# Retention attention and a SwiGLU FFN on one core: from two stages to six interleaved groups of 512 tokens

## The chip, the cores and the metric

The kernel runs on one NeuronCore of a Trainium2 chip. The metric is device time in microseconds (us) for one execution, lower is better. The engines are PE (TensorE, with its weight loads shown apart as PEld), DVE (VectorE), ACT (ScalarE), POOL (GpSimd) and SP (SyncE, which here only issues DMAs). Each takes its instructions in program order and waits on semaphores for the others.

## The reference

Inputs `q`, `k`, `v` have the shape (4, 8, 768, 64): 4 batches, 8 heads, 768 tokens, 64 per head, all float32. Weights are `w_gate` and `w_val` (512 x 1536), `w_out` (1536 x 512) and `rms_g` (512).

```python
# attention: a decayed linear recurrence per batch and head
gamma = 1.0 - 2.0 ** (-5.0 - np.arange(H))
for t in range(S):
    state = gamma[None, :, None, None] * state + einsum('bhd,bhe->bhde', k[:, :, t], v[:, :, t])
    y[:, :, t] = scale * einsum('bhd,bhde->bhe', q[:, :, t], state)
# x = y with the heads side by side: 3072 tokens x 512
rms = sqrt(mean(x * x, axis=-1, keepdims=True) + 1e-06)
xn = x / rms * rms_g
g = xn @ w_gate
out = (g * sigmoid(g) * (xn @ w_val)) @ w_out
```

The recurrence can be computed in chunks of 128 tokens: inside a chunk as a masked product of q and k with v, across chunks through a 64 x 64 state for each batch and head.

## The kernel before

It has two stages with a weight load between them.

**Attention (lines 96 to 163).** Two loops run over 4 batches and 8 heads. For each of the 32 pairs, SP loads q, k and v of all 768 tokens (192 KB each, in pieces of 256 bytes, lines 105 to 107). DVE scales and casts them to bf16 (L113 to L118), PE transposes q and k two chunks at a time (L126, L130) and DVE copies the results out of PSUM. Then six chunks of 128 tokens follow one another. For each, PE multiplies k and q (`a_ps`, L144), DVE applies the causal mask (`AmT`, L147), PE makes the output from the masked product and from the state (`y_ps`, L150 and L151), ACT copies it into `x_sbuf` (L154), and PE updates the state (`s_ps`, L159 and L160), which ACT scales by gamma^128 into the next `S_sb` (L162). So each chunk's state waits for that of the chunk before through PE and ACT. The matmuls here have 64 or 128 moving columns, and L144, L151 and L159 use 64 of the 128 rows of the array.

**Weights (lines 165 to 183).** The three weight matrices, 9.4 MB of float32, are loaded by SP after the attention loads; DVE casts them to bf16 and folds `rms_g` into the first two.

**FFN (lines 193 to 242).** A loop runs over 24 tiles of 128 tokens. ACT squares and sums (L198) and takes the root (L200), DVE normalises (L204), PE transposes (L209) and DVE copies (L210). For each of three groups of four blocks of d_ff, PE makes gate and value products with 128 moving columns (L220, L225), ACT applies Silu (L230), DVE multiplies (`sgv`, L232), and PE adds four 512-column matmuls to `out_ps` (L235). ACT copies the result (L241) and SP stores it (L242). The order between engines is that of a scheduler over the tile framework.

Of the kernel before, what the change touches and what calls it, by code (L numbers as in the profile page):

```python
# [9 lines left out]
F32 = mybir.dt.float32  # L10
BF16 = mybir.dt.bfloat16
# [6 lines left out]
def kernel(  # L18
# [11 lines left out]
    nc = tc.nc  # L30

    B, H, S, D = q.shape
    assert D == 64
    C = 128
    NCHUNK = S // C
    d_model = H * D
    n_tokens = B * S
    d_ff = moe_w_gate.shape[1]
    n_tiles = n_tokens // 128
    K_SUB = d_model // 128  # L40
    N_SUB = d_ff // 128

    scale = 1.0 / math.sqrt(D)
    gammas = [1.0 - 2.0 ** (-5.0 - h) for h in range(H)]

    const_pool = ctx.enter_context(tc.tile_pool(name="const", bufs=1))

    ident = const_pool.tile([128, 128], BF16)
    make_identity(nc, ident)

    ident_dup = const_pool.tile([D, 2 * D], BF16)
    nc.gpsimd.tensor_copy(ident_dup[:, :D], ident[:D, :D])
    nc.gpsimd.tensor_copy(ident_dup[:, D:], ident[:D, :D])  # L53

    causal = const_pool.tile([128, 128], BF16)
    nc.gpsimd.memset(causal, 1.0)
    nc.gpsimd.affine_select(
        out=causal,
        in_=causal,
        compare_op=mybir.AluOpType.is_ge,  # L60
        fill=0.0,
        base=0,
        pattern=[[1, 128]],
        channel_multiplier=-1,
    )

    iota_i = const_pool.tile([128, 1], mybir.dt.int32)
    nc.gpsimd.iota(iota_i, pattern=[[1, 1]], base=1, channel_multiplier=1)
    iota_f = const_pool.tile([128, 1], F32)
    nc.gpsimd.tensor_copy(iota_f, iota_i)  # L70

    bias_lnscale = const_pool.tile([128, 1], F32)
    nc.gpsimd.memset(bias_lnscale, math.log(scale))
    bias_zero = const_pool.tile([128, 1], F32)
    nc.gpsimd.memset(bias_zero, 0.0)

    gscale_q = const_pool.tile([128, H], F32)
    kscale = const_pool.tile([128, H], F32)
    for h in range(H):
        g = gammas[h]  # L80
        lng = math.log(g)
        nc.scalar.activation(
            gscale_q[:, h:h + 1], iota_f, AF.Exp, scale=lng, bias=bias_lnscale
        )
        nc.scalar.activation(
            kscale[:, h:h + 1], iota_f, AF.Exp, scale=-lng, bias=bias_zero
        )

    x_sbuf = const_pool.tile([128, n_tiles, d_model], BF16)

    NCO = NCHUNK // 2
    with (
        tc.tile_pool(name="work", bufs=5) as work_pool,
        tc.tile_pool(name="psum", bufs=2, space=bass.MemoryType.PSUM) as psum_pool,
    ):
      for b in range(B):
        for h in range(H):
            q_hbm = q[b, h].rearrange("(c p) d -> p c d", p=128)
            k_hbm = k[b, h].rearrange("(c p) d -> p c d", p=128)
            v_hbm = v[b, h].rearrange("(c p) d -> p c d", p=128)  # L100

            q_f = work_pool.tile([128, NCHUNK, D], F32, name="q_f")
            k_f = work_pool.tile([128, NCHUNK, D], F32, name="k_f")
            v_f = work_pool.tile([128, NCHUNK, D], F32, name="v_f")
            nc.sync.dma_start(out=q_f, in_=q_hbm)
            nc.sync.dma_start(out=k_f, in_=k_hbm)
            nc.sync.dma_start(out=v_f, in_=v_hbm)

            gC = gammas[h] ** C
            Qg = work_pool.tile([128, NCHUNK, D], BF16, name="Qg")  # L110
            Kg = work_pool.tile([128, NCHUNK, D], BF16, name="Kg")
            Vb = work_pool.tile([128, NCHUNK, D], BF16, name="Vb")
            nc.vector.tensor_scalar_mul(Qg, q_f, gscale_q[:, h:h + 1])  # L113
            nc.vector.tensor_scalar_mul(Kg, k_f, kscale[:, h:h + 1])
            nc.vector.tensor_copy(Vb, v_f)
            Kgd = work_pool.tile([128, NCHUNK, 2 * D], BF16, name="Kgd")
            nc.vector.tensor_copy(Kgd[:, :, :D], Kg)
            nc.vector.tensor_copy(Kgd[:, :, D:], Kg)  # L118

            Qg2 = Qg.rearrange("p (co c2) d -> p co (c2 d)", c2=2)  # L120
            Kg2 = Kg.rearrange("p (co c2) d -> p co (c2 d)", c2=2)
            QT = work_pool.tile([128, NCO, 128], BF16, name="QT")
            KT = work_pool.tile([128, NCO, 128], BF16, name="KT")
            for co in range(NCO):
                qp = psum_pool.tile([128, 128], BF16, name="qp")
                nc.tensor.transpose(qp, Qg2[:, co, :], ident)  # L126
                nc.vector.tensor_copy(QT[:, co, :], qp)
            for co in range(NCO):
                kp = psum_pool.tile([128, 128], BF16, name="qp")
                nc.tensor.transpose(kp, Kg2[:, co, :], ident)  # L130
                nc.vector.tensor_copy(KT[:, co, :], kp)  # L131

            S_sb = work_pool.tile([128, D], BF16, name="S_sb")
            nc.gpsimd.memset(S_sb, 0.0)

            for c in range(NCHUNK):
                co = c // 2
                po = (c % 2) * 64
                QgT = QT[po:po + 64, co, :]
                KgT = KT[po:po + 64, co, :]  # L140
                S_rhs = S_sb[po:po + 64, :]

                a_ps = psum_pool.tile([128, 128], F32, name="a_ps")
                nc.tensor.matmul(a_ps, KgT, QgT, start=True, stop=True)  # L144

                AmT = work_pool.tile([128, 128], BF16, name="AmT")
                nc.vector.tensor_mul(AmT, a_ps, causal)  # L147

                y_ps = psum_pool.tile([128, D], F32, name="y_ps")
                nc.tensor.matmul(y_ps, AmT, Vb[:, c, :], start=True, stop=False)  # L150
                nc.tensor.matmul(y_ps, QgT, S_rhs, start=False, stop=True)  # L151

                tile_idx = b * NCHUNK + c
                nc.scalar.copy(  # L154
                    x_sbuf[:, tile_idx, h * D:(h + 1) * D], y_ps
                )

                s_ps = psum_pool.tile([128, D], F32, name="s_ps")
                nc.tensor.matmul(s_ps, ident_dup, S_sb[:D, :], start=True, stop=False)  # L159
                nc.tensor.matmul(s_ps, Kgd[:, c, :], Vb[:, c, :], start=False, stop=True)  # L160
                S_new = work_pool.tile([128, D], BF16, name="S_sb")
                nc.scalar.mul(S_new, s_ps, gC)  # L162
                S_sb = S_new

    w_pool = ctx.enter_context(tc.tile_pool(name="weights", bufs=1))
    rms_g_sb = w_pool.tile([128, K_SUB], F32)
    for ks in range(K_SUB):
        nc.sync.dma_start(out=rms_g_sb[:, ks:ks + 1],
                          in_=moe_rms_g[ks * 128:(ks + 1) * 128][:, None])
    wg_f = w_pool.tile([128, K_SUB, d_ff], F32)  # L170
    wv_f = w_pool.tile([128, K_SUB, d_ff], F32)
    wo_f = w_pool.tile([128, N_SUB, d_model], F32)
    nc.sync.dma_start(out=wg_f, in_=moe_w_gate.rearrange("(k p) n -> p k n", p=128))
    nc.sync.dma_start(out=wv_f, in_=moe_w_val.rearrange("(k p) n -> p k n", p=128))
    nc.sync.dma_start(out=wo_f, in_=moe_w_out.rearrange("(n p) m -> p n m", p=128))

    wg_b = w_pool.tile([128, K_SUB, d_ff], BF16)
    wv_b = w_pool.tile([128, K_SUB, d_ff], BF16)
    for s in range(K_SUB):
        nc.vector.tensor_scalar_mul(wg_b[:, s, :], wg_f[:, s, :], rms_g_sb[:, s:s + 1])  # L180
        nc.vector.tensor_scalar_mul(wv_b[:, s, :], wv_f[:, s, :], rms_g_sb[:, s:s + 1])
    wo_b = w_pool.tile([128, N_SUB, d_model], BF16)
    nc.vector.tensor_copy(wo_b, wo_f)

    eps = 1e-6
    eps_tile = w_pool.tile([128, 1], F32)
    nc.gpsimd.memset(eps_tile, eps)

    ffnw = ctx.enter_context(tc.tile_pool(name="ffnw", bufs=4))
    ffnp = ctx.enter_context(tc.tile_pool(name="ffnp", bufs=2, space=bass.MemoryType.PSUM))  # L190
    outp = ctx.enter_context(tc.tile_pool(name="outp", bufs=2, space=bass.MemoryType.PSUM))

    for t in range(n_tiles):
        xt = x_sbuf[:, t, :]

        xsq = ffnw.tile([128, d_model], F32, name="xsq")
        sumsq = ffnw.tile([128, 1], F32, name="sumsq")
        nc.scalar.activation(xsq, xt, AF.Square, accum_out=sumsq)  # L198
        rstd = ffnw.tile([128, 1], F32, name="rstd")
        nc.scalar.activation(rstd, sumsq, AF.Sqrt, scale=1.0 / d_model, bias=eps_tile)  # L200
        nc.vector.reciprocal(rstd, rstd)
# [71 lines left out]
```

## Time and profile before

| | us |
|---|---|
| median of 3 runs (451.76 to 451.96) | 451.9 |
| span of the profiled execution (first to last instruction) | 449.7 |
| PE busy | 380.3 (85%) |
| PE weight loads busy | 247.8 (55%) |
| DVE busy | 209.9 (47%) |
| ACT busy | 191.9 (43%) |
| POOL busy | 6.6 (1%) |

The profile shows one execution. A busy share says how long at least one instruction of the engine was in flight; matmuls are pipelined, so a busy PE need not be PE at its peak rate, and the starts of successive matmuls say more. The page's slices cut the span into 40 equal parts of 11.24 us. In a row of grouped instructions stand line, engine, operation, tiles, shapes and count, then the total busy time in us, the mean of one in ns, the idle time before them in us, and what ended it. In the timeline, a row starts with the start and the duration in us.

### The profile page before, as it was taken

Reading aid. Unit: us, or ns where it says so; the run is one execution under the profiler, and the core shown is the slowest. Engines: PE = TensorE matmul, PEld = TensorE weight load, DVE = VectorE, ACT = ScalarE, POOL = GpSimd, SP = SyncE. Lnnn points to the kernel's source line nnn. Section 1 sums busy time; section 2 is a strip of 40 time slices with the busy share of each in tenths; the row PEclk is TensorE's granted clock in tenths of the full one; section 3 lists DMA queues with packets and bytes.
Section 4 is the critical chain, followed back from the end, with each engine's and each line's share of the span. In section 5 each row is a group of like instructions: output and inputs, shape, how many; then the busy total and the mean of one; then the engine's idle time right before and its main releaser. Section 6 shows DMA issues by size and latency. Waiting matters only on the chain.

```text
span 449.7 us, 9843 instructions
## 1 busy us (share of the span) xinstructions
PE 380.3 (85%) x3840; PEld 247.8 (55%) x3840; DVE 209.9 (47%) x769; ACT 191.9 (43%) x595; POOL 6.6 (1%) x47
## 2 busy tenths in 40 slices
PE   1888797888788878886389999999999999999995
PEld 0434343434343334333187777877787776767673
DVE  3566666656665666564656233242323333233221
ACT  4433364333333333335823156665674542222221
POOL 1000000000000000000000000000000000000000
PEclk9999999999999999999999999999999999999998
DMA  9964353443334331000991100100010001000010
GB/s 188 218 122 99 84 117 84 94 107 87 86 91 106 88 89 36 1 0 10 395 397 57 57 25 25 44 30 27 26 48 25 25 25 48 25 25 25 25 46 28
DMA packets 81951, 35.24 MB, mean 78 GB/s; under 512 B 76272, under 2 KB 76272, under 8 KB 81904
## 3 DMA queue, kind: packets, MB, share of 16 engines
q1 hardware_dynamic: 81904, 34.61, 29.6%
q8 instruction: 30, 0.49, 0.5%
q14 instruction: 17, 0.14, 0.1%
HBM read 28.31 MB, written 6.29 MB: 77 GB/s over the span
## 4 chain that ended last, share of the span: by engine, by line
PE 63%; ACT 12%; DVE 10%; DMA 7%; issue 5%; SPq 1%; POOL 1%; ACTq 0%; POOLq 0%; DVEq 0%
PE out_ps L235 15%; PE gT_ps L220 9%; PE vT_ps L225 9%; PE s_ps L159 7%; ACT S_sb L162 6%; PE s_ps L160 6%; DMA wo_f<-in_moe_w_out_dram 6%; DVE sgv L232 6%; PE y_ps L151 5%; PE y_ps L150 5%; ACT silu_g L230 4%; PE a_ps L144 4%; DVE AmT L147 2%; ACT x_sbuf L154 2%; PE qp L130 2%
## 5 line engine op out<-in xcount | busy, mean ns | idle before, releaser
L220 PE MATMUL gT_ps<-xnT,wg_b 128*128 128x128 bf16 x1152 | 110.3, 223 | 9.1 <-DVE wg_b L180 7.2
L225 PE MATMUL vT_ps<-xnT,wv_b 128*128 128x128 bf16 x1152 | 108.3, 219 | 0.1
L220 PEld LDWEIGHTS <-wg_b 128*128 128x128 bf16 x1152 | 80.8, 100 | 21.3 <-DVE wg_b L180 8.3
L230 ACT ACTIVATE silu_g<-gT_ps 128x512 bf16<-128x512 f32 x72 | 41.8, 597 | 98.9 <-PE gT_ps L220 93.1
L225 PEld LDWEIGHTS <-wv_b 128*128 128x128 bf16 x1152 | 77.1, 98 | 6.9 <-issue 0.2
L147 DVE TENSOR_TENSOR AmT<-a_ps,causal 128x128 bf16<-128x128 f32 x192 | 53.0, 290 | 52.5 <-PE a_ps L144 44.2
L235 PE MATMUL out_ps<-wo_b,sgv 128*128 128x512 bf16 x288 | 71.6, 381 | 6.4 <-DVE sgv L232 2.8
L232 DVE TENSOR_TENSOR sgv<-silu_g,vT_ps 128x512 bf16<-128x512 bf16 x72 | 48.3, 685 | 55.4 <-ACT silu_g L230 45.5
L159 PE MATMUL s_ps<-S_sb,ident_dup 64*128 64x64 bf16 x192 | 40.0, 208 | 35.9 <-ACT S_sb L162 24.3
L162 ACT ACTIVATE S_sb<-s_ps 128x64 bf16<-128x64 f32 x192 | 43.0, 224 | 62.4 <-PE s_ps L160 60.2
L154 ACT CAST x_sbuf<-y_ps 128x64 bf16<-128x64 f32 x192 | 40.5, 212 | 62.4 <-PE y_ps L151 59.6
L210 DVE COPY xnT<-tps 128x128 bf16<-128x128 bf16 x96 | 18.1, 219 | 77.3 <-PE tps L209 77.1
L160 PEld LDWEIGHTS <-Kgd 128*128 128x128 bf16 x192 | 20.2, 105 | 51.9 <-issue 48.5
L150 PE MATMUL y_ps<-Vb,AmT 128*128 128x64 bf16 x192 | 46.2, 240 | 1.5
L144 PE MATMUL a_ps<-QT,KT 64*128 64x128 bf16 x192 | 46.2, 288 | 0.0
L160 PE MATMUL s_ps<-Vb,Kgd 128*128 128x64 bf16 x192 | 45.3, 236 | 0.1
L151 PE MATMUL y_ps<-S_sb,QT 64*128 64x64 bf16 x192 | 44.6, 232 | 0.0
L235 PEld LDWEIGHTS <-sgv 128*128 128x128 bf16 x288 | 24.2, 97 | 34.6 <-DVE sgv L232 13.3
L150 PEld LDWEIGHTS <-AmT 128*128 128x128 bf16 x192 | 21.4, 111 | 32.5 <-DVE AmT L147 22.9
L126 PE MATMUL qp<-ident,Qg 128*128 128x128 bf16 x96 | 27.6, 293 | 6.4 <-DVE Qg L113 6.2
L159 PEld LDWEIGHTS <-ident_dup 64*128 64x128 bf16 x192 | 20.6, 107 | 15.7 <-POOL ident_dup L53 2.1
L131 DVE COPY KT<-qp 128x128 bf16<-128x128 bf16 x96 | 18.5, 221 | 22.5 <-PE qp L130 22.5
(43 smaller groups left out, 283.2 us busy)
## 6 DMA issues: line engine op xcount, KB each, us to landing
q_f<-in_q_dram SPq DMA_DIRECT2D x32, 192.0 KB, 2.5
k_f<-in_k_dram SPq DMA_DIRECT2D x32, 192.0 KB, 2.6
v_f<-in_v_dram SPq DMA_DIRECT2D x32, 192.0 KB, 2.6
out_dram<-out_sb SPq DMA_DIRECT2D x24, 256.0 KB, 2.0
wg_f<-in_moe_w_gate_dram SPq DMA_DIRECT2D x1, 3072.0 KB, 10.1
wv_f<-in_moe_w_val_dram SPq DMA_DIRECT2D x1, 3072.0 KB, 17.2
wo_f<-in_moe_w_out_dram SPq DMA_DIRECT2D x1, 3072.0 KB, 25.9
rms_g_sb<-in_moe_rms_g_dram SPq DMA_DIRECT2D x4, 0.5 KB, 2.1
```

What stands on the lines that cost most here:

```text
L144: nc.tensor.matmul(a_ps, KgT, QgT, start=True, stop=True)
L147: nc.vector.tensor_mul(AmT, a_ps, causal)
L150: nc.tensor.matmul(y_ps, AmT, Vb[:, c, :], start=True, stop=False)
L151: nc.tensor.matmul(y_ps, QgT, S_rhs, start=False, stop=True)
L159: nc.tensor.matmul(s_ps, ident_dup, S_sb[:D, :], start=True, stop=False)
L160: nc.tensor.matmul(s_ps, Kgd[:, c, :], Vb[:, c, :], start=False, stop=True)
L162: nc.scalar.mul(S_new, s_ps, gC)
L220: nc.tensor.matmul(gT_ps[:, nn, :], wg_b[:, s, n * 128:(n + 1) * 128], xnT[:, s, :], start=(s == 0), stop=(s == K_SUB - 1),)
L225: nc.tensor.matmul(vT_ps[:, nn, :], wv_b[:, s, n * 128:(n + 1) * 128], xnT[:, s, :], start=(s == 0), stop=(s == K_SUB - 1),)
L230: nc.scalar.activation(silu_g, gT_ps, AF.Silu)
L232: nc.vector.tensor_mul(sgv, silu_g, vT_ps)
L235: nc.tensor.matmul(out_ps, sgv[:, nn, :], wo_b[:, n, :], start=(n == 0), stop=(n == N_SUB - 1),)
```

## The change

The kernel body is rewritten, and the program order is now written out by hand (`manual_schedule`).

* The work is cut into six groups of 512 tokens: group c is chunk c (128 tokens) of all four batches, with all eight heads of a batch side by side in the 512 columns.
* Loads: one DMA of 256 KB for each of q, k, v of a (chunk, batch) pair, one group ahead, on SP, in pieces of 256 bytes. The weights are loaded by 11 DMAs on POOL's queue, issued before any attention work; they cast from float32 to bf16 on the way, so DVE's weight casts go. `rms_g` is broadcast to all partitions and applied in `piece_x`.
* The decays are folded into v (gamma^-t) and into the output (gamma^t), counted over the whole sequence, so the state is a plain sum and no chunk has a scaling step between PE and ACT.
* Casts of q, k and v to bf16 move to POOL. The root becomes a power of -0.5 on POOL. Transposed q and k of all heads leave PSUM in one ACT copy of 1024 columns; the mask and the output scaling are 512-column DVE operations. Pairs of heads share 128-wide tiles.
* Gate and value matmuls have 512 moving columns (four batches) with one 128 x 128 weight block each; `hT` holds all of d_ff for the group, and `down(b)` makes the output of one batch's 128 tokens from twelve 512-column matmuls.
* The FFN of group c is cut into 16 slots: 12 of `gv(n)` (8 matmuls) and 4 of `down(b)` (12 matmuls). After each slot's instructions, those of the next group's attention that `attention()` assigns to it are emitted. Group 0's attention is emitted alone ahead of the first FFN; the last group's FFN has no attention beside it.

```diff
+    ctx.enter_context(tc.manual_schedule())
+    loads = ctx.enter_context(tc.tile_pool(name="loads", bufs=5))
+    work = ctx.enter_context(tc.tile_pool(name="work", bufs=3))
+    ffw = ctx.enter_context(tc.tile_pool(name="ffw", bufs=3))
+    aps = ctx.enter_context(tc.tile_pool(name="aps", bufs=4, space=bass.MemoryType.PSUM))
+    fps = ctx.enter_context(tc.tile_pool(name="fps", bufs=4, space=bass.MemoryType.PSUM))
...
+            x = loads.tile([128, H, D], F32, name=name)
+            nc.sync.dma_start(
+                out=x, in_=src[b].rearrange("h (c p) d -> c p h d", p=C)[c])
...
+    for b in range(B):
+        load(0, b)
...
+    WB = 384
+    for i in range(DFF // WB):
+        sl = slice(i * WB, (i + 1) * WB)
+        nc.gpsimd.dma_start(out=wg_b[:, :, sl], in_=wg_v[:, :, sl])
+        nc.gpsimd.dma_start(out=wv_b[:, :, sl], in_=wv_v[:, :, sl])
+    for i in range(3):
+        sl = slice(i * 4, (i + 1) * 4)
+        nc.gpsimd.dma_start(out=wo_b[:, sl, :], in_=wo_v[:, sl, :])
+    def cast(c, b):
...
+        nc.gpsimd.tensor_copy(qb, q_f.rearrange("p h d -> p (h d)"))
+        nc.gpsimd.tensor_copy(kb, k_f.rearrange("p h d -> p (h d)"))
+        nc.gpsimd.tensor_tensor(
+            out=vp, in0=v_f, in1=vdec[:, c, :, None].to_broadcast([128, H, D]), op=ALU.mult)
...
+        if c + 1 < NCH:
+            load(c + 1, b)
+    def piece_t(c, b):
...
+                nc.tensor.transpose(qk_ps[:, i, hp, :], d[n][:, hp * 128:(hp + 1) * 128], ident)
+        nc.scalar.copy(qkT, qk_ps)
+    def piece_a(c, b):
...
+        for hp in range(NHP):
+            for i in range(2):
+                r = slice(i * 64, i * 64 + 64)
+                nc.tensor.matmul(a_ps[i][:, hp, :], d["kT"][r, hp, :], d["qT"][r, hp, :],
+                                 start=True, stop=True)
...
+        for i in range(2):
+            nc.vector.tensor_tensor(
+                out=am[:, i], in0=a_ps[i],
+                in1=causal[:, None, :].to_broadcast([128, NHP, 128]), op=ALU.mult)
+    def piece_y(c, b):
...
+                nc.tensor.matmul(y_ps[:, h, :], d["am"][:, i, hp, :], d["vp"][:, h, :],
+                                 start=first, stop=last, skip_group_check=True)
+        if c > 0:
+            for hp in range(NHP):
+                nc.tensor.matmul(y_ps[:, 2 * hp:2 * hp + 2, :], d["qT"][:, hp, :], st_b[b][:, hp, :],
+                                 start=False, stop=hp == NHP - 1, skip_group_check=True)
+        if c < NCH - 1:
...
+                nc.tensor.matmul(kv_ps[:, hp, :], d["kb"][:, sl],
+                                 d["vp"][:, 2 * hp:2 * hp + 2, :], start=True, stop=True)
+        nc.vector.tensor_tensor(
+            out=x, in0=y_ps, in1=ydec[:, c, :, None].to_broadcast([128, H, D]), op=ALU.mult)
+        nc.scalar.activation(xsq, x.rearrange("p h d -> p (h d)"), AF.Square,
+                             accum_out=cur[c, "ssq"][:, b:b + 1])
+        if c < NCH - 1:
+            for i in range(2):
...
+                    nc.vector.tensor_tensor(out=st_f[b][r], in0=st_f[b][r], in1=kv, op=ALU.add)
+                nc.gpsimd.tensor_copy(st_b[b][r, :, i * 64:i * 64 + 64], st_f[b][r])
+    def piece_rstd(c):
...
+        nc.gpsimd.tensor_scalar(out=ms, in0=ssq, scalar1=1.0 / DM, scalar2=1e-6,
+                                op0=ALU.mult, op1=ALU.add)
+        nc.gpsimd.tensor_tensor(out=rstd, in0=ms, in1=mhalf4, op=ALU.pow)
+    def piece_x(c, b):
...
+        nc.vector.scalar_tensor_tensor(
+            out=xn, in0=x.rearrange("p h d -> p (h d)"), scalar=cur[c, "rstd"][:, b:b + 1],
+            in1=g_bc, op0=ALU.mult, op1=ALU.mult)
...
+            nc.tensor.transpose(xt_ps[:, s, :], xn[:, s * 128:(s + 1) * 128], ident)
+        nc.vector.tensor_copy(cur[c, "xnT"][:, :, b * C:(b + 1) * C], xt_ps)
+    def attention(c):
+        s = [[] for _ in range(16)]
+        s[0].append(lambda: begin(c))
+        for b in range(B):
+            s[2 * b].append(lambda b=b: cast(c, b))
+            s[2 * b + 1].append(lambda b=b: piece_t(c, b))
+            s[2 * b + 2].append(lambda b=b: piece_a(c, b))
+            s[2 * b + 3].append(lambda b=b: piece_y(c, b))
+            s[12 + b].append(lambda b=b: piece_x(c, b))
+        s[10].append(lambda: piece_rstd(c))
+        return s
+    def ffn(c):
...
+        def gv(n):
...
+            for s in range(KS):
+                nc.tensor.matmul(g_ps, wg_b[:, s, sl], xnT[:, s, :], start=s == 0, stop=s == KS - 1)
...
+            for s in range(KS):
+                nc.tensor.matmul(v_ps, wv_b[:, s, sl], xnT[:, s, :], start=s == 0, stop=s == KS - 1)
...
+            nc.scalar.activation(sg, g_ps, AF.Silu)
+            nc.vector.tensor_tensor(out=hT[:, n, :], in0=sg, in1=v_ps, op=ALU.mult)
+        def down(b):
+            o_ps = fps.tile([128, DM], F32, name="o_ps", tag="ff")
+            for n in range(NFF):
+                nc.tensor.matmul(o_ps, hT[:, n, b * C:(b + 1) * C], wo_b[:, n, :],
+                                 start=n == 0, stop=n == NFF - 1)
...
+            nc.scalar.copy(o_sb, o_ps)
+            nc.sync.dma_start(out=out_v[c, b], in_=o_sb)
...
+    for sl in attention(0):
+        for f in sl:
+            f()
+    for c in range(NCH):
+        f_slots = ffn(c)
+        a_slots = attention(c + 1) if c + 1 < NCH else [[] for _ in range(16)]
+        for i in range(16):
+            f_slots[i]()
+            for f in a_slots[i]:
+                f()
```

More of the change, by code (lines that the diff above doesn't have):

```diff
@@ L49 @@
+    ident = const.tile([128, 128], BF16, name="ident")
     make_identity(nc, ident)
[L51 to L55, printed above, removed]
+    causal = const.tile([128, 128], BF16, name="causal")
     nc.gpsimd.memset(causal, 1.0)
     nc.gpsimd.affine_select(
[L58 to L65, printed above, removed]
@@ L79 @@
-    for h in range(H):
[L80 to L163, printed above, removed]
@@ L174 @@
[L174 to L182, printed above, removed]
@@ new lines @@
+    g_bc = const.tile([128, DM], F32, name="g_bc")
+    nc.sync.dma_start(out=g_bc, in_=moe_rms_g.partition_broadcast(128))
+    st_f = [const.tile([128, NHP, D], F32, name=f"st_f{b}") for b in range(B)]
+    st_b = [const.tile([128, NHP, 2 * D], BF16, name=f"st_b{b}") for b in range(B)]
+    for b in range(B):
+        nc.gpsimd.memset(st_b[b], 0.0)
+    wg_b = const.tile([128, KS, DFF], BF16, name="wg_b")
+    wv_b = const.tile([128, KS, DFF], BF16, name="wv_b")
+    wo_b = const.tile([128, NFF, DM], BF16, name="wo_b")
```

180 lines of the change are left out of this document (98 added, 82 removed).

## The prediction

> **What bounds the kernel now.** I read the busy line first, then the busy time by stage, then the chain that ended last and the waits.
>
> ```profile
> span 449.7 us, 9843 instructions
> PE 380.3 (85%) x3840; PEld 247.8 (55%) x3840; DVE 209.9 (47%) x769; ACT 191.9 (43%) x595; POOL 6.6 (1%) x47
> 10.00:210.00 200.00, 164.69 (x1146) 80.16 (x1144) 123.93 (x535) 79.87 (x391) 4.70 (x31) 1.00 0.41 86
> 213.00:239.00 26.00, 17.20 (x199) 14.44 (x200) 15.75 (x46) 13.51 (x39) 0.00 (x0) 1.00 0.94 364
> 239.00:446.00 207.00, 196.86 (x2493) 152.33 (x2490) 67.29 (x175) 90.92 (x141) 0.00 (x0) 1.00 0.08 31
> PE s_ps L159 <- ACT S_sb L162: 24.3, 91, 0.5
> DVE AmT L147 <- PE a_ps L144: 44.2, 66, 1.1
> 213.30 25.93 DMA wo_f<-in_moe_w_out_dram
> 446.02 0.58 ACT out_sb L241
> 446.63 0.33 SPq L242 DMA_DIRECT2D out_dram<-out_sb  x1
> ```
>
> The three rows by stage (start:end, length, then busy time and count of PE, PEld, DVE, ACT, POOL, the granted clock, DMA share, GB/s) say that there are three kernels in a row. Attention takes 210 us for some 1150 matmuls, one per 174 ns, with PE "busy" only because each lone matmul counts its whole latency: it hands over to ACT and DVE (the two wait rows) and gets the result back. Then the weights come, 26 us at 364 GB/s, with PE partly waiting. Then the FFN, 207 us with some 2490 matmuls and PE full. The granted clock is 1.00 throughout, so no stage is throttled. After the last matmul (446.0) come a copy and a store: 3.7 us to the span's end. The median, 451.9, lies 2.2 us over the span; I carry that 2.2.
>
> **What PE has to do afterwards.**
>
> ```profile
> 242.67 5.34 PE L235 MATMUL out_ps<-wo_b,sgv 128*128 128x512 bf16 x24
> L235 PE MATMUL out_ps<-wo_b,sgv 128*128 128x512 bf16 x288 | 71.6, 381 | 6.4 <-DVE sgv L232 2.8
> 337.01 0.83 PE L220 MATMUL gT_ps<-xnT,wg_b 128*128 128x128 bf16 x12
> L220 PE MATMUL gT_ps<-xnT,wg_b 128*128 128x128 bf16 x1152 | 110.3, 223 | 9.1 <-DVE wg_b L180 7.2
> 12.06 0.24 PE L160 MATMUL s_ps<-Vb,Kgd 128*128 128x64 bf16 x1
> 12.11 0.24 PE L150 MATMUL y_ps<-Vb,AmT 128*128 128x64 bf16 x1
> 12.28 0.23 PE L151 MATMUL y_ps<-S_sb,QT 64*128 64x64 bf16 x1
> 10.62 0.29 PE L144 MATMUL a_ps<-QT,KT 64*128 64x128 bf16 x2
> ```
>
> A matmul's own duration is latency; its price in a dense stream is the distance of starts. For 512 columns: (5.34 - 0.381) / 23 = 0.216 us. For 128 columns: (0.83 - 0.223) / 11 = 0.055. At 12.06 and 12.11 two full-height matmuls of 64 columns are 0.05 apart, so narrow ones cost the same 0.055; the one at 12.28, on 64 rows, starts 0.17 later: changing the tile's height costs some 0.12. Two 64-row matmuls on different halves (10.62) take together what one takes, so they run side by side.
>
> The Trainium skill, "TensorE: Matmul & The Clock Gate", Back-to-back issue gap, gives 131 ns a matmul as the sustained rate of weight-load and matmul pairs at 512 columns. By it the FFN below would be 73 us shorter. The row at 242.67 is such a stream and shows 216; the measurement decides, and I give that rule no chance.
>
> *FFN.* Per group 12 x 8 + 4 x 12 = 144 matmuls of 512 columns: 31.1 us; six groups 186.6. Widening gate and value from 4 x 0.055 = 0.22 to 0.216 brings almost nothing.
>
> *Attention on PE.* Per batch element: `piece_t` 8 x 0.055 = 0.44; `piece_a` four pairs and two height changes, 0.22 + 0.24 = 0.46; `piece_y` 12 matmuls 0.66 and 4 for the state 0.22; `piece_x` 4, 0.22. Together 2.0 us, 8.0 a group. Ends: no height change, 1.8; every one at the 0.17 of a height change, 6.1. I take 2.0 since 28 of 36 are full-height. Five groups lie in an FFN: 40 us, less 4 x 0.22 for the last, which makes no state.
>
> **Does the rest keep up?**
>
> ```profile
> L232 DVE TENSOR_TENSOR sgv<-silu_g,vT_ps 128x512 bf16<-128x512 bf16 x72 | 48.3, 685 | 55.4 <-ACT silu_g L230 45.5
> L147 DVE TENSOR_TENSOR AmT<-a_ps,causal 128x128 bf16<-128x128 f32 x192 | 53.0, 290 | 52.5 <-PE a_ps L144 44.2
> L210 DVE COPY xnT<-tps 128x128 bf16<-128x128 bf16 x96 | 18.1, 219 | 77.3 <-PE tps L209 77.1
> L230 ACT ACTIVATE silu_g<-gT_ps 128x512 bf16<-128x512 f32 x72 | 41.8, 597 | 98.9 <-PE gT_ps L220 93.1
> L154 ACT CAST x_sbuf<-y_ps 128x64 bf16<-128x64 f32 x192 | 40.5, 212 | 62.4 <-PE y_ps L151 59.6
> L198 ACT ACTIVATE xsq<-x_sbuf 128x512 f32<-128x512 bf16 x24 | 14.8, 618 | 0.0
> 0.80 0.20 POOL masks.py:197 MEMSET ident<- 128x128 bf16 x1 [0.29 <-POOLq L257]
> 1.66 0.23 POOL L52 COPY ident_dup<-ident 64x64 bf16<-64x64 bf16 x1
> L134 POOL MEMSET S_sb<- 128x64 bf16 x32 | 4.8, 151 | 196.0 <-ACT S_sb L162 161.4 <-PE a_ps L144 21.5 <-ACT x_sbuf L154 13.1
> ```
>
> *DVE:* 128 to 512 columns is 290 to 685 ns, 1.03 ns a column. Per group 12 `sgv`, 8 masks, 4 `x` at 0.69, 4 `xn` at about 0.69, 4 copies of 512 (0.219 + 384 x 1.03 = 0.61), 8 state sums of 256 columns (0.42): 25 us. *ACT:* 0.86 ns a column from L154 to L230, so the 1024-column copy takes 0.212 + 960 x 0.86 = 1.04; with 12 Silu, 4 squares and 4 output copies, 16 us. *POOL:* 0.83 ns a column from its memsets (204 against 151 ns for 64 more); a 512-column copy is 0.23 + 448 x 0.83 = 0.6. The two-input `vp` isn't shown: between 0.6 and twice that, and I take 1.2, for two inputs. With two state copies (0.39) a batch element costs 3.2, a group 13. A group lasts some 42 us, so none of the three is the bound; they'd be from 42 us a group on, for POOL 10.5 per batch element.
>
> Latency is another matter, as the pieces follow one another through engines that serve in order. From the start of `piece_y(b-1)`: `y_ps` ready 0.85, `x` on DVE to 1.64, square on ACT to 2.3, and behind it the copy of `qkT(b)` to 3.35. PE has finished the next `gv` at 3.1 and waits 0.3 for it. Silu of that `gv` stands behind the copy on ACT (to 3.95), `sgv` behind Silu (4.65), the two masks behind `sgv` (6.05); PE could start `piece_y(b)` at 5.7. So 0.67 is lost, three times a group: 2.0. At a group's end the first `gv` needs `xnT` whole: after the last transposes, 0.25 latency and the 0.61 copy: 0.9. Ends: nothing, if ACT and DVE come sooner; double, 5.8 a group. I take 2.9.
>
> So a group with attention beside it: 31.1 + 8.0 + 2.0 + 0.9 = 42.0; five: 210 less 0.9, 209.1. The last group: 31.1.
>
> **The start, which nothing hides.**
>
> ```profile
> 3.00:13.00 10.00, 3.77 (x25) 1.66 (x26) 4.54 (x20) 3.62 (x19) 0.00 (x0) 1.00 1.37 223
> 5.30 0.36 DVE L115 CAST Vb<-v_f 128x384 bf16<-128x384 f32 x1 [5.30 <-DMA v_f<-in_v_dram]
> 8.97 0.83 SPq L107 DMA_DIRECT2D v_f<-in_v_dram  x1
> q_f<-in_q_dram SPq DMA_DIRECT2D x32, 192.0 KB, 2.5
> q1 hardware_dynamic: 81904, 34.61, 29.6%
> ```
>
> Group 0 needs twelve loads, 3.15 MB, in the same 256-byte pieces that moved at 223 GB/s. The first three of before (0.59 MB) had landed at 5.3 us. Alone, all twelve land at 5.3 + 2.56 / 0.223 = 16.8. The weights are moved from after attention to the same time, on POOL's queue. Before, one queue carried all data, so no row shows sharing. Ends: 16.8, or all weights first, 16.8 + 25.9 = 42.7. By halves of the time, the 2.36 MB left at 6.2 us take 21 us: 27.
>
> POOL issues 11 weight DMAs ahead of its first cast. No row shows a DMA issued by POOL; SP needs up to 0.83 us for one. Ends: 0.43 (the quickest SP issue) and four times 0.83. I take twice, 1.7: 19 us from about 5, so POOL is free at 24, and four rounds of casts (4 x 2.4 + 3 x 0.8 = 12) end at 36. That is later than the landing at 27, so POOL's queue sets the start. Then for the last batch element `piece_y` 0.9, `x` 0.7, square 0.8, the two POOL steps 0.4, and four `piece_x` one behind another, each 0.69 + 0.47 + 0.61 = 1.8: 7.1. FFN starts at 36 + 9.9 = 46. By then some 8 of the 9.4 MB have landed, and `w_out` is needed only 25 us later. Cheapest: 16.8 + 1.2 + 9.9 = 28. Dearest: POOL free at 42, cast at 54: 64.
>
> The Trainium skill, "DMA: Bandwidth & Descriptors", Queues, rings and completion order, says that each DMA engine takes turns between queues by packets of several descriptors. If those carry about equal bytes, q, k and v move at 1 / (1/223 + 1/364) = 138 GB/s, the last lands at 23, and the sum would be 12 lower where POOL isn't late. No run so far shows it.
>
> **The sum.** 46 + 209.1 + 31.1 + 3.7 = 289.9 span; with 2.2, **292 us**. Gone: attention's 210 becomes 40 of PE plus 46 at the start, and the weights' 26 lie under that start.
>
> **Rivals.**
> 1. *POOL issues cheaply and the waits are covered.* For it: ACT 16 and DVE 25 of 42 us leave room, SP issues in 0.43 to 0.83. Landing at 23 to 27 then sets the start (34 to 38) and the 2.9 a group shrink: 292 - 10 - 10 = 272. Against: in-order queues.
> 2. *The start is longer, or the small matmuls dearer.* POOL at 3.3 us a DMA: 64, so 310; small matmuls at half way to 6.1 add 20 x 2 = 40: 332.
> 3. *The interleaving doesn't interleave*: each piece waits its full chain, 6 us a batch element in place of 0.67: 20 x 5.4 = 108 more, 400. Against: the pieces stand one `gv` (1.73 us) apart, and each single step takes 0.7 to 1.05.
> 4. *Slower than before: the casting weight DMA is slow.* After the last weights land, 10.4 (down of group 0) + 168 + 31.1 + 5.9 = 215 us are left, so it ends above 452 from a landing at 237, a rate under 40 GB/s. Against: the poorest row here, 256-byte pieces, moves 223, and these pieces are 1536 and 2048 bytes. At half of 223 the weights land at 90 and it ends at 305.
>
> **How the numbers follow.** Forecast 0.65; rival 1: 0.17; rival 2: 0.12; rival 3: 0.04; rival 4: 0.02. Range 262 to 330: rival 1 with 10 to spare for waits that vanish entirely, and nearly all of rival 2. About 0.2% of this kernel's time (0.9 us) is what its measurement can tell from no change; all cases but the last are far faster: faster 0.97, same 0.01, slower 0.02.
>
> **What would show it.** PE nearly full from about 46 us on, with 512-column starts 0.216 apart and no granted clock under 1; a period of 42 us from one group's first `gv` to the next; PE's waits naming `qkT` (ACT), `am` (DVE) and, at group ends, `xnT`; in the start, POOL's casts behind its DMA issues. It is wrong if PE waits for weights, if POOL's issue rows are far from 1.7, if the attention matmuls' busy time per batch element is far from 2 us, or if a group's period isn't 40 to 45.

## The result and the profile after

| | before | after |
|---|---|---|
| median, us | 451.85 | 300.95 (300.7 to 301.65, 4 runs) |
| ratio, 95% interval | | 0.6664 [0.6654, 0.6673] |
| span of the profiled execution, us | 449.7 | 299.4 |

The forecast was 292, with a range of 262 to 330. The sum, term by term (after: starts of the first `gv` of each group, from the timeline below):

| term | predicted | measured | difference |
|---|---|---|---|
| first `gv` of group 0 | 46 | 59.26 | +13.3 |
| five groups with attention beside them | 209.1 | 204.81 | -4.3 |
| last group | 31.1 | 31.25 | +0.1 |
| after the last matmul | 3.7 | 4.1 | +0.4 |
| outside the span | 2.2 | 1.55 | -0.65 |
| sum | 292 | 300.95 | +8.9 |

The busy line of the page, after:

```profile
span 299.4 us, 4437 instructions
PE 242.3 (81%) x1696; PEld 122.8 (41%) x1696; DVE 141.1 (47%) x232; ACT 100.0 (33%) x186; POOL 91.2 (30%) x153
```

Busy time by stage, after (start:end, length, then PE, PEld, DVE, ACT, POOL, granted clock, DMA share, GB/s):

```profile
0.00:18.00 18.00, 0.00 (x0) 0.00 (x0) 0.00 (x0) 4.44 (x17) 11.46 (x29) 1.00 1.11 180
18.00:43.00 25.00, 8.88 (x90) 6.41 (x91) 8.19 (x15) 4.97 (x9) 9.62 (x17) 1.00 1.21 193
59.00:62.00 3.00, 2.75 (x7) 0.99 (x7) 0.20 (x1) 0.60 (x1) 0.00 (x0) 1.00 1.35 218
100.00:140.00 40.00, 38.69 (x288) 19.77 (x286) 23.38 (x41) 15.60 (x28) 13.89 (x22) 1.00 0.50 106
```

From 60 us on PE is full, and the attention's 210 us of before are gone into it. What is left over stands in the first two rows: 43 us in which PE does 8.9 us of work while the DMA engines are full (shares above 1: packet times of several queues overlap). The third row lies at the start of the FFN and is used further down.

The timeline of PE, after (start, duration, in brackets the wait before it):

```profile
59.26 1.86 PE L248 MATMUL g_ps<-xnT,wg_b 128*128 128x512 bf16 x4 [0.52 <-DVE xnT L219]
60.91 1.91 PE L251 MATMUL v_ps<-xnT,wv_b 128*128 128x512 bf16 x4
...
66.57 1.03 PE L251 MATMUL v_ps<-xnT,wv_b 128*128 128x512 bf16 x4
...
102.25 1.04 PE L248 MATMUL g_ps<-xnT,wg_b 128*128 128x512 bf16 x4 [0.52 <-DVE xnT L219]
...
113.32 0.40 PE L154 MATMUL a_ps<-qkT 64*128 64x128 bf16 x8 [0.22 <-ACT qkT L144]
...
115.74 0.38 PE L171 MATMUL y_ps<-vp,am 128*128 128x64 bf16 x7 [0.16 <-DVE am L158]
115.96 0.39 PE L176 MATMUL y_ps<-st_b,qkT 128*128 128x128 bf16 x4
...
264.07 1.04 PE L248 MATMUL g_ps<-xnT,wg_b 128*128 128x512 bf16 x4 [0.52 <-DVE xnT L219]
...
284.80 10.52 PE L259 MATMUL o_ps<-wo_b,hT 128*128 128x512 bf16 x48
```

The first group takes 43.0 us (59.26 to 102.25), the next four 161.8 together, 40.5 each. A dense 512-column matmul still costs (1.03 - 0.379) / 3 = 0.217. PE's waits, after (waited for: us in total, times, longest):

```profile
PE qk_ps L142 <- POOL qb L129: 24.4, 2, 19.0
PE xt_ps L218 <- DVE xn L213: 8.7, 4, 4.1
PE a_ps L154 <- ACT qkT L144: 6.7, 11, 1.2
PE y_ps L171 <- DVE am L158: 5.9, 21, 0.9
PE g_ps L248 <- DVE xnT L219: 3.1, 6, 0.5
```

The last three rows are the tiles that the prediction named. The first two belong to group 0 alone: two waits for a cast `qb` and four for `xn`. The group-end wait stands in six equal pieces of 0.52 us. One batch element's round trip shows why `qkT` and `am` are late. The timeline of ACT, after:

```profile
111.65 0.63 ACT L188 ACTIVATE xsq<-x 128x512 f32<-128x512 bf16 x1 [1.66 <-DVE x L185]
...
112.28 0.99 ACT L144 COPY qkT<-qk_ps 128x1024 bf16<-128x1024 bf16 x1
113.17 0.60 ACT L253 ACTIVATE sg<-g_ps 128x512 bf16<-128x512 f32 x1
```

The copy ends at 113.27 and PE goes on at 113.32; Silu follows the copy, `hT` on DVE follows Silu, the masks follow `hT`: the queueing of the prediction, with the square just ahead of the copy.

**The start.** The chain that ended last, after, between 24 and 51 us (start, duration, what):

```profile
24.07 17.99 DMA k_f<-in_k_dram
...
42.18 0.62 POOL kb L130
...
49.51 1.06 POOL rstd L207
...
50.59 1.10 DVE xn L213
```

The timeline of POOL, after:

```profile
9.54 0.80 POOL L116 DMA_DIRECT2D wv_b<-in_moe_w_val_dram  x1
...
17.57 0.74 POOL L119 DMA_DIRECT2D wo_b<-in_moe_w_out_dram  x1 [1.96 <-DMA wg_b<-in_moe_w_gate_dram]
18.30 0.62 POOL L129 CAST qb<-q_f 128x512 bf16<-128x512 f32 x1
...
40.52 0.61 POOL L129 CAST qb<-q_f 128x512 bf16<-128x512 f32 x1 [5.00 <-DMA q_f<-in_q_dram]
```

POOL is free at 18.3, and later it is POOL that waits 5.0 us for a load. The last k of group 0 lands at 42.06, and the last v just before its cast at 42.99. The view of the DMA queues over 12 to 36 us, after (packets, MB, share of 16 engines; q0 is POOL's queue with the weights, counted as the bf16 bytes written, q1 is SP's):

```profile
q0 software_dynamic: 4364, 3.51, 91.0%
q1 hardware_dynamic: 4369, 1.10, 34.6%
```

Each queue had the same number of packets, but 3.51 MB / 4364 = 804 bytes against 1.10 / 4369 = 252. So q, k and v moved at 1.10 / 24 = 46 GB/s as long as weights were in flight, against 223 alone.

### The profile page after: what moved, and what is told of

It is laid out like the page before. It is cut to its first block, busy times and chain, and to the rows that moved or that the text cites. A ratio compares the mean times of both kernels' runs of the same rounds, so it can differ in the third digit from the quotient of the medians.

```text
span 299.4 us, 4437 instructions
## 1 busy us (share of the span) xinstructions
PE 242.3 (81%) x1696; PEld 122.8 (41%) x1696; DVE 141.1 (47%) x232; ACT 100.0 (33%) x186; POOL 91.2 (30%) x153
## 4 chain that ended last, share of the span: by engine, by line
PE 53%; DVE 17%; ACT 9%; SPq 8%; DMA 6%; issue 5%; POOL 1%; DVEq 0%; ACTq 0%; POOLq 0%
PE o_ps L259 21%; PE g_ps L248 13%; PE v_ps L251 12%; SPq L62 8%; DVE am L158 7%; DMA k_f<-in_k_dram 6%; DVE hT L254 4%; ACT xsq L188 3%; DVE x L185 3%; ACT qkT L144 3%; ACT sg L253 3%; PE xt_ps L218 2%; PE y_ps L171 2%; DVE xn L213 1%; DVE xnT L219 1%
## 5 line engine op out<-in xcount | busy, mean ns | idle before, releaser
L254 DVE TENSOR_TENSOR hT<-sg,v_ps 128x512 bf16<-128x512 bf16 x72 | 49.5, 688 | 72.5 <-PE v_ps L251 45.4
L248 PE MATMUL g_ps<-xnT,wg_b 128*128 128x512 bf16 x288 | 75.9, 387 | 3.1 <-DVE xnT L219 3.1
L251 PE MATMUL v_ps<-xnT,wv_b 128*128 128x512 bf16 x288 | 74.9, 383 | 0.0
L259 PE MATMUL o_ps<-wo_b,hT 128*128 128x512 bf16 x288 | 65.6, 379 | 0.0
L253 ACT ACTIVATE sg<-g_ps 128x512 bf16<-128x512 f32 x72 | 43.0, 597 | 63.9 <-PE g_ps L248 63.9
L158 DVE TENSOR_TENSOR am<-a_ps,causal 128x512 bf16<-128x512 f32 x48 | 30.8, 682 | 33.5 <-PE a_ps L154 33.5
L251 PEld LDWEIGHTS <-wv_b 128*128 128x128 bf16 x288 | 28.5, 99 | 35.0 <-issue 1.7
L259 PEld LDWEIGHTS <-hT 128*128 128x128 bf16 x288 | 27.5, 98 | 30.4
L248 PEld LDWEIGHTS <-wg_b 128*128 128x128 bf16 x288 | 25.5, 99 | 29.1 <-DVE xnT L219 3.5
L131 POOL TENSOR_TENSOR vp<-v_f,vdec 128x512 bf16<-128x512 f32 x24 | 26.8, 1117 | 8.7 <-DMA v_f<-in_v_dram 5.5
```

Source lines behind the costliest of these rows:

```text
L131: nc.gpsimd.tensor_tensor(out=vp, in0=v_f, in1=vdec[:, c, :, None].to_broadcast([128, H, D]), op=ALU.mult)
L158: nc.vector.tensor_tensor(out=am[:, i], in0=a_ps[i], in1=causal[:, None, :].to_broadcast([128, NHP, 128]), op=ALU.mult)
L248: nc.tensor.matmul(g_ps, wg_b[:, s, sl], xnT[:, s, :], start=s == 0, stop=s == KS - 1)
L251: nc.tensor.matmul(v_ps, wv_b[:, s, sl], xnT[:, s, :], start=s == 0, stop=s == KS - 1)
L253: nc.scalar.activation(sg, g_ps, AF.Silu)
L254: nc.vector.tensor_tensor(out=hT[:, n, :], in0=sg, in1=v_ps, op=ALU.mult)
```

## The experiments

Theory A: the shared DMA engines set the start (q, k and v land late). Theory B, the prediction's: POOL's queue sets it. Runs 2 and 12 show how the engines are shared.

**1. The weight DMAs behind group 0's casts** (eight DMAs in place of eleven).

```diff
-    WB = 384
-    for i in range(DFF // WB):
...
-    for sl in attention(0):
+    for i, sl in enumerate(attention(0)):
         for f in sl:
             f()
+        if i == 6:
+            load_weights()    # WB = 512, w_out in 2 pieces
```

> The weights' DMAs (eight in place of eleven) are issued by POOL only after the casts of group 0, so q, k and v of group 0 have the DMA engines to themselves. Theory A (the start is DMA time: 14 us for q, k, v of group 0 at 223 GB/s plus 26 us for the weights at 364 GB/s, and the weights were served first): the last of group 0 lands at 17 to 20 in place of 42, the first gv starts at 33 to 38 in place of 59.3, total 277 (270 to 284). Theory C (the same 40 us of DMA time must pass before the FFN can run, whatever the order): the first gv starts early but PE then waits for wg_b, wv_b or wo_b, total 295 to 302.

278.71 us, ratio 0.6167 [0.615, 0.6185]. PE's timeline in it:

```profile
37.76 1.86 PE L249 MATMUL g_ps<-xnT,wg_b 128*128 128x512 bf16 x4 [0.52 <-DVE xnT L220]
```

The first `gv` comes 21.5 us sooner and the time is 22.2 lower. PE waits for no weight in it, so theory C falls. The start is now group 0's own round trips: ACT's copies of `qkT` stand 5.0 us apart (11.69, 16.67, 21.65). The run moves POOL's issues and the sharing together, so it doesn't tell A from B alone; the next does.

**2. Eight weight DMAs, still in front.** Fewer issues on POOL, the same bytes.

```diff
-    WB = 384
+    WB = 512
...
-    for i in range(3):
+    for i in range(2):
```

> Eight weight DMAs in place of eleven, at the old place: POOL no longer waits for an earlier DMA before it issues the last three, and its first cast comes at 11 in place of 18.3 us. Theory B (the prediction's step: POOL's queue sets the start): total 7 lower, 294. Theory A (DMA time sets it; the last q and k land at 40 to 42 either way): within 1.5 of 301.

299.94 us, 0.6653 [0.6629, 0.6678]. POOL's timeline in it:

```profile
10.43 0.70 POOL L131 CAST qb<-q_f 128x512 bf16<-128x512 f32 x1
...
38.23 1.04 POOL L133 TENSOR_TENSOR vp<-v_f,vdec 128x512 bf16<-128x512 f32 x1 [6.02 <-DMA v_f<-in_v_dram]
```

POOL casts 7.9 us earlier, then waits for the loads, and the first `gv` is at 58.38: 0.9 sooner for 7.9. The interval overlaps that of the changed kernel. Theory B falls. Its queues over 12 to 36 us:

```profile
q0 software_dynamic: 3755, 3.75, 91.7%
q1 hardware_dynamic: 3755, 0.95, 29.9%
```

With the gate and value pieces a third longer (999 bytes a packet in the mean, for 804) the counts are again equal, and SP's rate falls from 46 to 40 GB/s: turns go by packets, not by bytes.

**3. No interleaving**: the next group's pieces all behind the FFN's 16 slots.

```diff
         for i in range(16):
             f_slots[i]()
+        for i in range(16):
             for f in a_slots[i]:
                 f()
```

> All attention of the next group is emitted after the 16 FFN slots in place of between them; the same instructions. Theory A (the gain is that attention's latency lies beside FFN matmuls): attention alone takes some 5 us a batch element and 13 us at its end, 33 a group, against 8 to 10 beside the FFN: 5 x 23 = 115 more, total 405 to 425. Rival (the gain is the rewritten attention itself: no state scaling between PE and ACT, wide tiles, 36 matmuls a batch element): total 301 to 320.

423.18 us (one run, no interval). Its busy time by stage:

```profile
60.00:92.00 32.00, 31.85 (x141) 14.10 (x141) 8.36 (x13) 8.92 (x15) 0.00 (x0) 1.00 0.06 20
92.00:125.00 33.00, 14.19 (x148) 10.15 (x147) 16.61 (x28) 7.09 (x13) 13.90 (x22) 0.58 0.56 109
```

A group takes 65 us: 32.5 of FFN and 32.4 of attention, the latter with PE busy for 14 of 33 us at a granted clock of 0.58. Without interleaving the kernel takes 122 us more, of the 151 gained. The lower clock in these stretches has a part in it (four transposes take up to 0.63 us, against 0.39 at full clock); how large, no run shows. Interleaving is what turns 32 us of hand-overs into 9 of PE's time.

**4. No weight DMAs at all.** It leaves out the weights' load: they are constants written by DVE.

```diff
-    WB = 384
-    for i in range(DFF // WB):
...
+    nc.vector.memset(wg_b, 0.01)
+    nc.vector.memset(wv_b, 0.01)
+    nc.vector.memset(wo_b, 0.01)
```

> The weights are set to a constant by DVE in place of the 11 DMAs; nothing else is changed. Theory A: the last of group 0 lands at 17, the first gv starts at 31 to 36, total 273 to 278; it is the floor for any order of the loads. If POOL or the latencies set the start and not the DMAs, total 290 or more.

290.18 us (one run). The timeline of DVE in it:

```profile
14.95 5.18 DVE L114 MEMSET wo_b<- 128x6144 bf16 x1 [1.23 <-issue]
20.04 1.22 DVE L153 TENSOR_TENSOR am<-a_ps,causal 128x512 bf16<-128x512 f32 x2
```

By its number this is the rival's "290 or more", but the edit put a new delay in: three fills of some 5 us stand ahead of the first mask on DVE. Run 1 tells how much: there the first mask is at 8.32, 11.7 us sooner, and the first `gv` at 37.76, 11.2 sooner than the 48.96 here. So without the fills the first `gv` would stand at about 37 (an estimate from the two runs), where run 1 has it: with the loads out of the way group 0's round trips are the floor, not theory A's 31 to 36.

**5. All gate and value matmuls in 128 columns again**, to test that the 512-column form brings almost nothing.

```diff
             for s in range(KS):
-                nc.tensor.matmul(g_ps, wg_b[:, s, sl], xnT[:, s, :], ...)
+            for b in range(B):          # for v_ps too
+                t = slice(b * C, (b + 1) * C)
+                for s in range(KS):
+                    nc.tensor.matmul(g_ps[:, t], wg_b[:, s, sl], xnT[:, s, t], ...)
```

> Gate and value matmuls with 128 moving columns again (four for each one of 512; 2304 instructions in place of 576), all else as in the changed kernel. The prediction's working: 0.22 for four against 0.216, 576 x 0.005 = 3 us more, total 302 to 306. Rival (the wide form is a main part of the gain, through weight loads that do not hide behind 128 columns, or because ends of groups lie differently): 310 or more.

298.71 us, 0.6618 [0.6608, 0.6628]: faster than the changed kernel, where slower was expected. PE's timeline in it:

```profile
64.05 1.06 PE L250 MATMUL g_ps<-xnT,wg_b 128*128 128x128 bf16 x16
64.94 1.06 PE L255 MATMUL v_ps<-xnT,wv_b 128*128 128x128 bf16 x16
```

Sixteen narrow ones take 0.89 against 0.864 for four wide ones (3% dearer; 2% was expected). But the first narrow ones need only batch 0's slice of `xnT`, which is ready well before: the wait for `xnT` at the group's end (3.1 us in all) is gone from the list. The expectation had left that out.

**6. The square behind the next Silu**: off ACT's path to `qkT`.

```diff
-        nc.scalar.activation(xsq, x..., AF.Square, ...)   # in piece_y
+            s[2 * b + 4].append(lambda b=b: piece_sq(c, b))
-        s[10].append(lambda: piece_rstd(c))
+        s[11].append(lambda: piece_rstd(c))
```

> The square of each batch element is emitted one slot later, behind the next slot's Silu, so that the copy of qkT on ACT no longer stands behind it. Theory A (ACT's order is what PE waits for: some 0.5 us a batch element, three times a group in five groups): 5 to 8 less, total 293 to 296. Rival (DVE's order, sgv ahead of the masks, holds PE as well and the wait only moves): within 2 of 301.

292.48 us, 0.6478 [0.6466, 0.649], half a microsecond below the range of theory A. From PE's waits in it:

```profile
PE a_ps L154 <- ACT qkT L144: 4.5, 4, 1.2
...
PE y_ps L171 <- DVE am L158: 3.5, 6, 0.9
```

Of 11 and 21 waits 4 and 6 are left, group 0's. A period is 39.05 instead of 40.5: the square's place cost 1.4 us a group.

**7. `piece_x` one slot earlier**, so that the last `xnT` is ready before the group's end.

```diff
-            s[12 + b].append(lambda b=b: piece_x(c, b))
+            s[11 + b].append(lambda b=b: piece_x(c, b))
```

> piece_x of every batch element one slot earlier, so that the last copy into xnT lies beside the last down and the next group's first gv need not wait for it. Theory A (0.5 to 0.7 us at each of five group ends): 2.5 to 3.5 less, total 297.5 to 298.5. Rival (PE then waits for rstd or xn at the earlier place): 301 or more.

313.32 us, 0.6944 [0.693, 0.6958]: 12 us slower than the changed kernel, as the rival had it. The timeline of PE in it:

```profile
135.22 0.40 PE L218 MATMUL xt_ps<-ident,xn 128*128 128x128 bf16 x4 [2.39 <-DVE xn L213]
135.45 4.27 PE L259 MATMUL o_ps<-wo_b,hT 128*128 128x512 bf16 x12
...
179.29 0.40 PE L218 MATMUL xt_ps<-ident,xn 128*128 128x128 bf16 x4 [2.39 <-DVE xn L213]
179.53 2.75 PE L259 MATMUL o_ps<-wo_b,hT 128*128 128x512 bf16 x12
```

And its busy time by stage:

```profile
136.00:140.00 4.00, 4.00 (x16) 1.73 (x14) 0.74 (x2) 0.24 (x1) 1.64 (x2) 0.57 0.00 0
179.00:183.00 4.00, 3.71 (x24) 1.94 (x25) 1.78 (x5) 0.58 (x1) 2.71 (x3) 1.00 0.00 0
```

The moved transposes stand in PE's queue ahead of `down(0)` and wait 2.39 us for `xn` in four groups, 1.51 in the last. After three of the four waits the granted clock drops (0.57 in the mean of the first row), and twelve matmuls take 4.27 us instead of 2.75. After the one at 179.29 it stays at 1.00. The five periods add up to 217 us, 12 more than in the changed kernel. The period with the wait alone is 1.9 us longer than there (42.4), and two with the lower clock behind it are 3.5 longer (44.0 and 44.1). So a wait there costs itself and, most times, the clock behind it.

**8. Root and `piece_x` of group 0 for each batch as it comes.**

```diff
+            else:                       # c == 0
+                s[2 * b + 4].append(lambda b=b: piece_rstd1(c, b))
+                s[2 * b + 4].append(lambda b=b: piece_x(c, b))
```

> In group 0 alone, the root and piece_x are done for each batch element as soon as its output is there, in place of all four after the last: three of the four piece_x (2.1 us each) no longer lie behind the last load. Theory A: 5 to 6.5 less, total 294.5 to 296. Rival (POOL's in-order queue holds: each root waits behind casts that wait for loads, or casts wait behind roots): 0 to 3 less.

309.62 us, 0.6858 [0.6842, 0.6875]: slower, which neither expectation had. DVE's timeline in it:

```profile
45.05 0.75 DVE L221 SCALAR_TENSOR_TENSOR xn<-x,rstd,g_bc 128x512 bf16<-128x512 bf16 x1 [19.27 <-DMA g_bc<-in_moe_rms_g_dram]
```

The `xn` that was moved forward needs `g_bc`, whose DMA stands on SP behind the twelve late loads. DVE, in order, waits 19 us, PE behind it; the first `gv` is at 68.3, 9.0 later, as the time is 8.7 higher. So it tests the order of SP's queue and not what was meant.

**9. Only the first `gv` of each group in 128 columns.**

```diff
+            cols = [slice(b * C, (b + 1) * C) for b in range(B)] if n == 0 else [slice(0, GT)]
...
+            for t in cols:
+                for s in range(KS):
+                    nc.tensor.matmul(g_ps[:, t], wg_b[:, s, sl], xnT[:, s, t], ...)
```

> Only the first gv of each group has 128 moving columns, one batch after the other; the other eleven keep 512. Theory A (all gate and value matmuls narrow gained because the first one then needs only batch 0's slice of xnT, so the 0.52 us wait at the end of each group goes): 2.5 to 3.5 less than the changed kernel, total 297.5 to 298.5. Rival (the narrow matmul itself is cheaper in this stream): under 0.5 less, total 300.5 or more.

296.37 us, 0.6561 [0.6542, 0.6579]: lower than expected. The period falls from 40.5 to 39.9, 0.6 in each of five groups, and the start's half-rate phase (below) is shorter: the first two `gv` take 4.6 us instead of 6.0. It is 2.3 us below run 5: what narrow matmuls cost in the other eleven `gv`.

**10. Runs 1, 6 and 9 together.** The edits are those three.

> The weights after the casts of group 0, the square one slot later, and the first gv of each group narrow, all else as in the changed kernel. If the three are independent: 278.7 - 8.5 - 2.5 = 267.7 (266 to 269). Rival (with the waits gone another engine's order becomes the bound, or the FFN of group 0 now catches up with the weights): 271 or more.

267.31 us, 0.5908 [0.5896, 0.592], as expected. The period is 38.4 us. The three gains alone add to 22.2 + 8.5 + 4.6 = 35.3; together they give some 34.

**11. As run 10, with group 0 pipelined** over its batches, and the weight DMAs two at a time between its steps.

```diff
+    cast(0, 0)
+    piece_t(0, 0)
+    cast(0, 1)
+    piece_a(0, 0)
+    piece_t(0, 1)
+    ...
+    piece_rstd1(0, 0)
+    load_weights(0)
+    piece_y(0, 1)
+    piece_x(0, 0)
+    ...
```

> As the three together, and group 0 is emitted as a pipeline: transposes and scores of the next batch element ahead of the output of this one, root and piece_x of each batch element one step behind it, weight DMAs two at a time between. Theory A (with the loads out of the way the start is the in-order chain, 5 us a batch element and 12 us at its end, of which DVE needs only 4.25 a batch element): the first gv starts at 27 to 31 in place of 37.8, total 258 to 262. Rival (POOL's in-order queue, with weight DMAs and roots between the casts, or the weights coming later, holds it): 265 or more.

266.88 us, 0.5906 [0.5898, 0.5915]: no change against run 10 that these intervals can tell, and not the 258 to 262 of theory A. The timeline of POOL and PE in it:

```profile
33.57 1.91 PE L262 MATMUL g_ps<-xnT,wg_b 128*128 128x128 bf16 x16
...
49.74 0.61 POOL L131 CAST kb<-k_f 128x512 bf16<-128x512 f32 x1 [3.11 <-DMA k_f<-in_k_dram]
50.41 0.40 PE L143 MATMUL qk_ps<-ident,kb 128*128 128x128 bf16 x4 [1.16 <-POOL kb L131]
```

The first `gv` comes 2.6 us sooner than in run 10 (36.20), and the first group takes 43.4 us instead of 41.5: group 1's loads now lie beside the weights (3099 packets of SP's queue to 3119 of POOL's from 30 to 50 us), POOL's casts wait for them and PE for the casts. Most of the gain is lost again to the sharing of the DMA engines.

**12. Four of group 0's loads on ACT's queue.** If turns go by packets, a second queue gives the loads two turns in three.

```diff
+    BY_ACT = [("k_f", 2), ("v_f", 2), ("q_f", 3), ("v_f", 3)]
...
-            nc.sync.dma_start(
+            if c > 0 or (name, b) not in BY_ACT:
+                nc.sync.dma_start(
...
+    for name, b in BY_ACT:              # behind the exponentials
+        nc.scalar.dma_start(out=raw[0, b][i], in_=...)
```

> Four of group 0's last six loads (k and v of batch 2, q and v of batch 3) are issued by ACT, behind its 16 exponentials that end at 5.5 us, instead of by SP. Theory T (the DMA engines take one packet from each queue in turn, so that in the changed kernel from 12 to 36 us POOL's queue and SP's each had some 4,367 packets, of 804 and of 252 bytes): with three queues the packet counts in a stretch such as 12 to 20 us are equal one by one, q, k and v together get two turns in three. By the packet times that follow (18.6 ns for a small one alone, 3,440 in 4 us over 16 engines; 88 ns for a round of two, so 69 for a weight packet) a round takes 106 ns and q, k and v move at about 77 instead of 46 GB/s; the 2 MB open at 8 us land at about 34 instead of 42, and the first gv stands at 51 to 53 instead of 59.3; time 293 to 295. Theory W (weights first, whatever the number of load queues): no load lands earlier, first gv 58 to 60, 299 to 302. Theory S (SP's and ACT's loads share one turn): the counts of the two together equal POOL's; 299 to 302 too. If ACT is held at its own queue past 20 us, its first copy of qkT is late and the first gv comes later than 60.

292.81 us, 0.6474 [0.6447, 0.6502]; first `gv` at 52.76, as theory T had it. The queues in it, 12 to 20 us (q10 is ACT's):

```profile
q0 software_dynamic: 1310, 0.97, 77.6%
q1 hardware_dynamic: 1310, 0.33, 31.2%
q10 hardware_dynamic: 1309, 0.33, 18.5%
```

The three queues have one packet each in turn: q, k and v move at 0.66 / 8 = 82 GB/s, beside all the weights, issued in front by POOL as in the changed kernel. Theory W (weights first) and theory S (one turn for both load queues) fall. One step of the expectation was off: ACT was held at its fourth DMA until 22.1, and its first copy of `qkT` came at 22.12 instead of 20.18, yet the first `gv` did not come later than 60. From that copy on, the round trips of group 0 between ACT, DVE and PE set the pace, 5 us a batch element, with POOL's casts done at 35.7.

## Why the prediction was right, and where it was off

**Right: what takes attention's place.** PE is full from the first `gv` on, 0.217 us a matmul but for the first twelve, the granted clock at 1.00, and a period of 40.5 us lies in the 40 to 45 that was given. The last group measured 31.25 for 31.1. DVE, ACT and POOL are busy for 23.4, 15.6 and 13.9 of 40 us (predicted 25, 16, 13 of 42): none is the bound. Run 3 shows that the order of emission does it.

**Slightly over: the group.** Attention's matmuls were put at 2.0 us a batch element. By starts they take 0.33 for `piece_a` (113.32 to the next `gv` at 113.65; predicted 0.46; that leaves some 0.05 for a height change, for which I had 0.12) and 0.69 for `piece_y` with the state (0.88): a full-height matmul of 64 columns costs 0.22 / 7 = 0.031 (115.74 to 115.96), not the 0.055 that I took for all narrow ones. With 0.44 and 0.22 for the rest that is 1.7, or 6.7 a group. So 40.5 - 31.2 - 6.7 = 2.6 are lost to waits, for which I had 2.9. Runs 6 and 9 divide them: 1.4 through the square ahead of `qkT`, 0.6 at the group's end (`xnT`'s copy takes 0.43, not 0.61). With both removed the period is 38.4, 0.5 above the sum of the matmuls. The widening to 512 columns is worth 3% of `gv`, as said, but its wide first `gv` must wait for all four batches, a cost that I did book (0.9) without seeing that it belongs to the width.

**The step that failed: "POOL's queue sets the start".** I took POOL free at 24 and its casts done at 36, later than a landing at 27. POOL's issues cost 0.78 each, not 1.7, and with the holds before the last three it was free at 18.3. By my own sign ("far from 1.7") the step was wrong. The last k landed at 42.06, near the end of my bound that I had called all weights first (42.7). The wrong step was sharing "by halves of the time". The engines take turns by packets, and a packet of q is 252 bytes against 804. The casts end at 44.0 instead of 36: 8.0 of the 13.3. Run 2 shows that POOL isn't it, runs 2 and 12 show the turns. The Trainium skill, "DMA: Bandwidth & Descriptors", Queues, rings and completion order, says that each engine alternates between queues at packet boundaries. These counts agree with it (4364 to 4369, 3755 to 3755, 1310 to 1310 to 1309); whether a turn is one such packet or several in a row they don't show. What failed is the "about equal bytes" that I added to that rule: it gave a landing at 23.

The other 5.3 us lie in the tail behind the casts, 15.2 us (44.0 to 59.26) where 9.9 was booked. I had the last `vp` cast end it all, but the last `kb` goes through transposes, copy, `a_ps` and the masks until 46.57: 2.5. The two POOL steps of the root take 1.4, not 0.4 (1.06 for one power of 128x4): 1.0. Four `piece_x` take 8.7, not 7.1, with `xn` at 0.74 to 1.53 instead of 0.69: 1.6. And 0.2 in between.

**What was luck.** That 292 lies within 3% of 300.95 is in part luck: the start came out 13.3 us longer, by a cause that I had wrong, and the five groups 4.3 shorter, which took part of it back. The range of 262 to 330 held either cause of a longer start, so a time inside it doesn't bear out my account of the start.

**The first group** is 2.5 us longer than the others: its first twelve wide matmuls run at half rate (59.26 to 60.91, 0.41 each). Nothing in the prediction had that.

**The rivals.** Rival 1 (cheap issues on POOL) had the issues right and the landing wrong. Rival 2 (a longer start) is what happened in size, 59 against its 64, by another cause. Rival 3 did not come, but its 108 us more is near the 122 that run 3 takes where nothing is interleaved. Rival 4 fails: the weights were through by some 40 us.

## What to carry to other kernels

When two queues share the DMA engines, compare the packet sizes: turns were taken by the packet here, so the queue with 256-byte pieces got a fifth of its lone rate (46 of 223 GB/s) beside a queue with longer ones. Issue the long ones later (22 us here), or put the short ones on two queues (8 us).
For pieces emitted between other work, list each in-order engine's queue at that place: one 0.6 us square ahead of a copy cost 1.4 us a group, and a piece moved forward is late if any operand's DMA stands at the end of a queue.

## What the runs showed of the hardware beyond that

* **A half-rate phase that the clock column doesn't show.** After the thin matmuls of the start, twelve 512-column matmuls come 0.41 to 0.43 us apart, then 0.217, while the granted clock reads 1.00. The Trainium skill, "TensorE: Matmul & The Clock Gate", Part 1, gives 426.7 ns cold and 215.7 warm for 512 columns, and warns that the trace's clock events can be unreliable. Both agree with these rows; its 131 ns (Back-to-back issue gap) does not, here as before.
* **A lower clock after a short gap.** In run 7 three of four equal waits of 2.39 us were followed by a granted clock of 0.50 for some 3 us, the fourth was not, so the gap alone does not decide it. The same page, Why this matters for your kernels, names gaps above some 3 us; here shorter ones went with it.
* **`xn` on DVE** takes 0.74 in the median and up to 1.64; the long ones seen lie beside casts on POOL. The Trainium skill, "SBUF — State Buffer", SBUF: two separate sides, says that a DVE operation with two SBUF inputs and a POOL operation that reads SBUF exclude each other. That fits; no run here took the casts away to show it.
* **Issuing can hold an engine.** POOL waited 1.7 to 2.1 us before each of its last three weight DMAs, after eight, and the profile names an earlier weight DMA as what it waited for. ACT was held at its fourth in run 12 until 22.1, when a load that SP had issued landed. Whether the queues or the program's own waits set this limit, no run shows.
